# Attention, feed-forward layer and gated mixing on one core: conversion slots at 0.6 a step beside the second batch's attention, the next quarter's from the attention's end

## The chip, the cores and the metric

The kernel runs on one core of a Trainium2 chip. The metric is device time in microseconds (us): the median of the runs of the whole kernel. Work is done by five engines with a queue of instructions each, which they take in order: PE (TensorE, matrix products), DVE (VectorE), ACT (ScalarE), POOL (GpSimd) and SP, which here only starts transfers. An instruction that waits holds up everything behind it on its engine.

## The reference

B=2 batches, H=8 heads, S=768 positions, D=64, so a model width of 512. Three layers follow each other:

```
# 1 attention: window of 16 to each side, and a summary of each block of 32 keys
k_sum, v_sum = max and mean of k, v over each block of 32
scores = [q k^T / 8 where |i-j| < 16, else -1e9 ; q k_sum^T / 8 + log 32]
x = softmax(scores) [v ; v_sum]                  # (B, S, 512)
# 2 feed-forward, inner width 2048
u = x + (x^T U V)^T                              # U 768x32, V 32x768
x = u + relu(u w_ch1) w_ch2
# 3 gated mixing, inner width 1024, x_prev = x moved on by one position
xk, xr = mu_k x + (1-mu_k) x_prev, mu_r x + (1-mu_r) x_prev
out = sigmoid(xr w_r) * (relu(xk w_k)^2 w_v)
```

The weights lie in the memory of the chip as 64-bit floats and are brought to 32 bits on the chip.

## The kernel before, in words

**The order of the work.** The heads go in pairs n = 0 to 7. Pairs 0 to 3 are batch 0, pairs 4 to 7 batch 1. The attention of batch 0 fills the start (to about 54 us). Then the attention of batch 1 (`tail`) runs interleaved with the feed-forward layer of batch 0 over the first quarter of the inner width (`first_units`; `both` takes two steps of the attention for one of the feed-forward). This ends near 126 us. Then comes the first quarter for batch 1 alone (to 168 us), the quarters q = 1 to 3 for both batches (to about 364 us), and the third layer.

**The feed-forward layer.** A quarter has four blocks i of 128 inner columns, and each batch two chunks c of 384 positions. `f1` (L494) makes hidden block i: 12 matmuls (L506), a relu on ACT that gives the high part hh (L512), and on DVE the low part hl (L514), which is put in `hid_late` and emitted at the next `hid_flush`. `f2` (L520) multiplies hidden block i into four accumulators (L532); after the quarter's last block DVE adds them to y (L540, L543), and POOL adds the low part of u (`y_rest`, L308). Each product is made of three: high part by high, high by low, low by high. f1 and f2 each give way once in the middle (`yield`) and once at the end; a piece of six matmuls between two such points is called a step.

**The conversions.** Each weight block of 128 x 512 comes from memory as pairs of 32-bit words and passes five stages (`conv_jobs`, L399): s1 two ACT instructions (L423, L424), s2 three on DVE (L429, L432, L433), s3 an add on POOL (L439), s4 the high part whi on ACT (L464), s5 the low part wlo (L468), on DVE or POOL as the block says (`put_w`, `quarter_blocks`). In the first quarter DVE makes the low parts of all four blocks of w_ch2 and of blocks 2 and 3 of w_ch1; in the others POOL makes them all. A load goes on SP's queue. The stages stand in slots of a list `side`: a slot is one call that emits the next stages of the blocks under way, and a block takes two slots. The blocks of the first quarter are named below w1.0 to w1.3 and w2.0 to w2.3.

**What sets the order around the change.** There is no scheduler: the engines' queues hold what the Python code emits, in its order. `run(gen, rate)` (L744) walks a chain of steps and takes `rate` slots from `side` after each. In the attention a table `plan` (L316 to L397) says at which tick which part is emitted; its entries are "k" (`k_prep`: block maxima ks of the keys on DVE, L137, and the key windows kw on POOL, L143 to L145), "sv" (`sum_v`: block sums vs on DVE, L153; L158 on PE turns them, ACT copies them out at L160, POOL into vcat at L161), "d" (take slots from `side`), "u" (the feed-forward layer's input u, with its low part ulo on DVE, L301), and others. `drain(side)` without a number empties the list at once.

```
    run(both(first, tail, 2, 1), 1.0)
    for _ in tail:
        pass
    drain(side)
    ...
    side.extend(conv_jobs(quarter_blocks(1, wb_p)))
    run(chain(ffn_unit(0, 1, 0), ffn_unit(0, 1, 1)), 0.6)
    drain(side)
```

## Time and profile before

| what | value |
|---|---|
| time, median of 3 runs | 540.93 us (539.65 to 541.06) |
| time of the profiled execution | 540.89 us |
| its span, first to last instruction | 539.1 us |
| mean granted clock of PE | 0.991 |
| busy: PE, DVE, ACT, POOL | 515.4, 317.6, 250.4, 203.4 us |
| PE on the chain that ended last | 79% of the span |

The sum below is made against the profiled execution's own time, 540.89 us, of which 1.8 us lie around the span; it stands 0.04 us under the median of the runs. A busy PE can be at full or at half its clock: the granted clock of a stretch is 1.00 or 0.50, or between when the stretch holds both; the two levels are 2.4 and 1.2 GHz.

### The profile page before, as it was taken

To read this page: it belongs to the slowest core of one execution; us is meant where nothing else is said; L and a number is where in the kernel's file an instruction comes from. 1 tells how busy PE (TensorE), PEld (TensorE's weight loads), DVE (VectorE), ACT (ScalarE), POOL (GpSimd) and SP (SyncE) were. 2 spreads that over 40 slices of the span, in tenths; PEclk is the share of its full clock that TensorE was granted. 3 is DMA by queue.
4 is the path that set the end of the run, shared out by engine and by line. 5 is a ranking of instruction groups with operands and counts; after the bars stand their busy time and mean duration, and the time that the engine had idled before them with its cause. 6 is when DMAs were issued, how large, how long until landed. Compare 5 with 4: busy or idle time off the path is not lost.

```text
span 539.1 us, 8921 instructions
## 1 busy us (share of the span) xinstructions
PE 515.4 (96%) x3468; PEld 471.1 (87%) x3468; DVE 317.6 (59%) x706; ACT 250.4 (46%) x532; POOL 203.4 (38%) x184
## 2 busy tenths in 40 slices
PE   5889799999998999999999999999999999999997
PEld 4567577789998999999999999999888888888885
DVE  5995996444684486747775366565867443542222
ACT  4985674533451345524453254543566533532221
POOL 6553543032668166635765064232532120120000
PEclk9989898999999999999999999999999999999999
DMA  8995530400332133323433032021201000100101
GB/s 310 307 318 135 197 104 0 126 1 1 117 125 71 40 118 117 122 74 110 126 117 118 0 119 79 0 79 39 79 0 39 21 1 9 51 0 1 60 0 58
DMA packets 15129, 45.71 MB, mean 85 GB/s; under 512 B 2656, under 2 KB 2912, under 8 KB 15088
## 3 DMA queue, kind: packets, MB, share of 16 engines
q1 hardware_dynamic: 14912, 44.92, 25.2%
q8 instruction: 27, 0.44, 0.3%
q10 hardware_dynamic: 144, 0.18, 0.2%
q14 instruction: 14, 0.11, 0.1%
q0 software_dynamic: 32, 0.05, 0.0%
HBM read 42.00 MB, written 3.15 MB: 84 GB/s over the span
## 4 chain that ended last, share of the span: by engine, by line
PE 79%; DVE 10%; ACT 3%; DMA 3%; POOL 3%; issue 1%; SPq 0%; DVEq 0%; ACTq 0%; POOLq 0%
PE acc L532 23%; PE gen L506 22%; PE gen L648 12%; PE acc L670 12%; PE gen L632 5%; DMA stg<-vb 2%; PE gen L240 1%; DVE A L433 1%; POOL A L439 1%; DVE C L432 1%; DVE P L212 1%; DVE C L429 1%; DMA kt<-kt 1%; POOL wlo L468 1%; PE gen L227 1%
## 5 line engine op out<-in xcount | busy, mean ns | idle before, releaser
L439 POOL TENSOR_TENSOR A<-C,A 128x512 int32<-128x512 int32 (+1 forms) x54 | 71.4, 1322 | 89.2 <-DVE A L433 87.3
L532 PE MATMUL acc<-hh,whi 128*128 128x384 f32 x256 | 87.9, 343 | 2.6 <-DVE y L540 2.6
L506 PE MATMUL gen<-uhi,whi 128*128 128x384 f32 x256 | 87.8, 343 | 1.2 <-DVE hl L514 0.8
L506 PE MATMUL gen<-uhi,wlo 128*128 128x384 f32 x256 | 86.9, 340 | 0.0
L506 PE MATMUL gen<-ulo,whi 128*128 128x384 f32 x256 | 86.9, 340 | 0.0
L532 PE MATMUL acc<-hh,wlo 128*128 128x384 f32 x256 | 86.5, 338 | 0.0
L532 PE MATMUL acc<-hl,whi 128*128 128x384 f32 x256 | 86.5, 338 | 0.0
L468 POOL TENSOR_TENSOR wlo<-A,whi 128x512 fp32r<-128x512 f32 x46 | 68.0, 1478 | 37.4 <-ACT whi L464 37.3
L512 ACT ACTIVATE hh<-gen 128x384 fp32r<-128x384 f32 x64 | 31.3, 490 | 108.5 <-PE gen L506 108.4
L514 DVE SCALAR_TENSOR_TENSOR hl<-gen,hh 128x384 fp32r<-128x384 f32 x64 | 35.5, 555 | 65.0 <-ACT hh L512 65.0
L652 DVE TENSOR_TENSOR kt<-kt 128x384 f32<-128x384 f32 x32 | 20.3, 635 | 64.6 <-ACT kt L651 64.6
L433 DVE SCALAR_TENSOR_TENSOR A<-stg,A 128x512 int32<-128x512 int32 (+1 forms) x54 | 55.9, 1036 | 0.0
L532 PEld LDWEIGHTS acc<-hh,whi 128*128 128x128 f32 x256 | 48.1, 188 | 4.5 <-ACT hh L512 2.1
L506 PEld LDWEIGHTS gen<-uhi,whi 128*128 128x128 f32 x256 | 48.4, 189 | 2.8 <-DVE hl L514 1.4
L506 PEld LDWEIGHTS gen<-ulo,whi 128*128 128x128 f32 x256 | 48.5, 189 | 0.3 <-DVE ulo L301 0.3
L506 PEld LDWEIGHTS gen<-uhi,wlo 128*128 128x128 f32 x256 | 48.6, 190 | 0.0
L532 PEld LDWEIGHTS acc<-hl,whi 128*128 128x128 f32 x256 | 48.1, 188 | 0.0
L532 PEld LDWEIGHTS acc<-hh,wlo 128*128 128x128 f32 x256 | 48.1, 188 | 0.0
L464 ACT CAST whi<-A 128x512 fp32r<-128x512 f32 x52 | 32.2, 620 | 27.5 <-POOL A L439 27.3
L429 DVE TENSOR_SCALAR C<-C 128x512 f32<-128x512 f32 (+1 forms) x54 | 30.5, 565 | 23.0 <-ACT C L424 21.7
L648 PE MATMUL gen<-xkl,whi 128*128 128x384 f32 x128 | 43.2, 338 | 0.6 <-POOL xkl L610 0.6
L648 PE MATMUL gen<-xkh,whi 128*128 128x384 f32 x128 | 43.2, 337 | 0.0
(127 smaller groups left out, 985.8 us busy)
## 6 DMA issues: line engine op xcount, KB each, us to landing
stg<-w SPq DMA_DIRECT2D x32, 512.0 KB, 3.3
stg<-wk SPq DMA_DIRECT2D x8, 512.0 KB, 3.3
stg<-wv SPq DMA_DIRECT2D x8, 512.0 KB, 3.3
vcat<-vw SPq DMA_DIRECT2D x7, 585.0 KB, 4.7
kt<-kt SPq DMA_DIRECT2D x8, 384.0 KB, 5.3
vt<-vt SPq DMA_DIRECT2D x8, 384.0 KB, 5.7
out<-sig SPq DMA_DIRECT2D x12, 256.0 KB, 2.1
qt<-qt SPq DMA_DIRECT2D x7, 384.0 KB, 6.2
```

Of the source, the lines that this page charges most:

```text
L429: nc_v.tensor_scalar(out=c_f, in0=c_f, scalar1=as_float(0x38000000), scalar2=as_float(0x47EFFE00), op0=ALU.max, op1=ALU.min)
L433: nc_v.scalar_tensor_tensor(out=a, in0=st[i]["raw"][:, :, 1], scalar=-2 ** 31, in1=a, op0=ALU.bitwise_and, op1=ALU.bitwise_or)
L439: nc_p.tensor_tensor(out=a, in0=c, in1=a, op=ALU.add)
L464: nc_s.copy(wt[key][0], w)
L468: eng.tensor_tensor(out=lo, in0=w, in1=hi.bitcast(F32), op=ALU.subtract)
L506: nc_t.matmul(ps, w[:, sl], x[:, k], start=(n == 0), stop=(n == 3 * KD - 1))
L512: nc_s.activation(hh, ps, AF.Relu)
L514: lambda: nc_v.scalar_tensor_tensor(out=hl, in0=ps, scalar=0.0, in1=hh.bitcast(F32), op0=ALU.max, op1=ALU.subtract)
L532: nc_t.matmul(acc[d], w[:, sl], x, start=(i == 0 and n == 0), stop=(i == FT - 1 and n == 2))
L632: nc_t.matmul(ps, x[:, k, sl], w, start=(n == 0), stop=(n == 3 * KD - 1))
L648: nc_t.matmul(ps, w[:, sl], x[:, k], start=(n == 0), stop=(n == 3 * KD - 1))
L670: nc_t.matmul(acc, x[:, sl], w, start=(f == 0 and n == 0), stop=(f == KFT - 1 and n == 2))
```

## The change

In the attention of batch 0, the two single slots at ticks 10 and 11 move into the hand-written end of that attention, one ahead of u of pair 2 (`m`) and one behind the key preparation of pair 4, which itself moves there with its `sum_v`. Beside the attention of batch 1 the rate falls from 1.0 to 0.6 slots a step, and the list is not emptied at its end. The conversions of the second quarter are queued in `end_attention`, so that they follow in the same list without a gap, and what is left at the end of a quarter runs over into the next; the list is emptied once, after the last quarter. So that a block can't be read before it is converted, `f1` and `f2` call `ready`, which takes slots until the low part of their block has been emitted. `hold` stops the taking of slots in the second half of a unit's last `f2`. The low parts of w2.0 to w2.3 move from DVE to POOL. `hid_flush` runs at every step. `y_rest` of the first quarter goes between the conversions of quarter 2, whose rate is 0.75 in place of 0.5.

```diff
-    "g2", n), ("u", m, 1), ("fl",), ("ffn",), ("u", n, 0), ("u", n, 1), ("fl",),
+    ("t", n, 2), ("v", n, 1), ("g2", m), ("fl",), ("v", n, 2), ("fl",), ("d", 1), ("u", m, 0), ("g", n),
+    ("k", n + 1), ("d", 1), ("ffn",), ("g2", n), ("u", m, 1), ("fl",), ("sv", n + 1), ("ffn",), ("u", n, 0),
+    ("u", n, 1), ("fl",),
...
-                (10, (("lt", 5), ("d", 1))), (11, (("lv", 4), ("d", 1))),
-                (12, (("lv", 5), ("k", 4), ("sv", 4))),
+                (10, (("lt", 5),)), (11, (("lv", 4),)),
+                (12, (("lv", 5),)),
...
             eng.tensor_tensor(out=lo, in0=w, in1=hi.bitcast(F32), op=ALU.subtract)
+            done.add(key)
...
             res.append(block("w1", f, ("w1", f), pool, nc_v if q == 0 and i > 1 else nc_p))
-            res.append(block("w2", f, ("w2", f), pool, nc_v if q == 0 else nc_p))
+            res.append(block("w2", f, ("w2", f), pool))
...
     def f1(q, b, c, i, keep=False):
         hid_flush()
+        ready(("w1", q * FT + i))
...
     def f2(q, b, c, i):
         hid_flush()
+        ready(("w2", q * FT + i))
...
             if d == 2:
+                hold[0] = i == FT - 1
                 yield
...
+        hold[0] = False
         if i == FT - 1:
...
-                    side.append(lambda b=b, c=c, d=d: y_rest(b, c, d))
+                    rest.append(lambda b=b, c=c, d=d: y_rest(b, c, d))
...
+    def ready(key):
+
+        while key not in done:
+            drain(side, 1)
...
     def run(gen, rate):
         due = 0.0
         for _ in gen:
+            hid_flush()
             due += rate
-            while due >= 1.0:
+            while due >= 1.0 and not hold[0]:
...
     def end_attention():
         a_p.release()
         pools["y", 1] = tc.alloc_tile_pool(name="y1", bufs=1, side="right")
+        pools["wb"] = tc.alloc_tile_pool(name="wb", bufs=16, side="right")
         y_stage(1)
+        side.extend(conv_jobs(quarter_blocks(1, pools["wb"])))
...
-    run(both(first, tail, 2, 1), 1.0)
+    run(both(first, tail, 2, 1), 0.6)
     for _ in tail:
         pass
-    drain(side)
...
-    side.extend(conv_jobs(quarter_blocks(1, wb_p)))
     run(chain(ffn_unit(0, 1, 0), ffn_unit(0, 1, 1)), 0.6)
-    drain(side)
     for q in range(1, FQ):
...
-            side.extend(conv_jobs(blocks + [wk_block(4 * (q - 1) + f) for f in range(4)]))
-            run(chain(*units), 0.5)
+            for k, job in enumerate(conv_jobs(blocks + [wk_block(4 * (q - 1) + f) for f in range(4)])):
+                side.append(job)
+                if q == 2 and k % 2 and rest:
+                    side.append(rest.pop(0))
+            if q == 2:
+                side.extend(rest)
+            run(chain(*units), 0.5 if q == 1 else 0.75)
...
-        drain(side)
+    drain(side)
```

PE's order is the same in both kernels; what moves is what the other engines do for it. Three places show it. Line numbers of the changed kernel are a few higher (L439 becomes L440, L468 becomes L470, L532 becomes L538, L464 becomes L466, L512 becomes L516).

DVE where the first batch's attention ends and the second's begins (near 54 us), before:

```order
L280 TENSOR_TENSOR gst<-acc,gst 32x128
L301 TENSOR_TENSOR ulo<-acc,uhi 128x384 x4
L137 TENSOR_REDUCE ks<-kt_111 128x24
L153 TENSOR_REDUCE vs<-vt_113 128x24
L429 TENSOR_SCALAR C<-C 128x512
L432 TENSOR_SCALAR C<-C 128x512
L433 SCALAR_TENSOR_TENSOR A<-stg,A 128x512
L514 SCALAR_TENSOR_TENSOR hl<-gen,hh 128x384
L468 TENSOR_TENSOR wlo<-A,whi 128x512
L514 SCALAR_TENSOR_TENSOR hl_944<-gen,hh_943 128x384
L212 ISA P,nm<-gen,mask 128x120
```

and after:

```order
L430 TENSOR_SCALAR C<-C 128x512
L433 TENSOR_SCALAR C<-C 128x512
L434 SCALAR_TENSOR_TENSOR A<-stg,A 128x512
L137 TENSOR_REDUCE ks<-kt_111 128x24
L280 TENSOR_TENSOR gst<-acc,gst 32x128
L301 TENSOR_TENSOR ulo<-acc,uhi 128x384 x2
L153 TENSOR_REDUCE vs<-vt_113 128x24
L301 TENSOR_TENSOR ulo<-acc,uhi 128x384 x2
L518 SCALAR_TENSOR_TENSOR hl<-gen,hh 128x384
L518 SCALAR_TENSOR_TENSOR hl_938<-gen,hh_937 128x384
L430 TENSOR_SCALAR C<-C 128x512
L433 TENSOR_SCALAR C<-C 128x512
```

The two reductions of pair 4 (L137, L153) now stand between the parts of u, a conversion's three instructions ahead of them, and no low part (L468) is left here.

POOL at the last pair of the attention (near 107 us), before; here wlo_1344 of w2.3 doesn't occur, because DVE makes it:

```order
L439 TENSOR_TENSOR A_1153<-C_1154,A_1153 128x512
L439 TENSOR_TENSOR A_1234<-C_1235,A_1234 128x512
L161 COPY vcat0_104<-vm_1398 24x24x64
L143 COPY kw1_109<-kt1_111 128x12x32
L144 COPY kw1_109<-kt1_111 128x12x64
L145 COPY kw1_109<-ks_1407 128x12x24
L161 COPY vcat1_105<-vm_1610 24x24x64
L311 TENSOR_TENSOR y_919<-y_919,ulo_593 128x384 x4
```

and after; wlo_1492 is that of w2.2, wlo_1591 that of w2.3:

```order
L145 COPY kw1_109<-ks_1389 128x12x24
L440 TENSOR_TENSOR A_1319<-C_1320,A_1319 128x512
L470 TENSOR_TENSOR wlo_1492<-A_1319,whi_1491 128x512
L440 TENSOR_TENSOR A_1422<-C_1423,A_1422 128x512
L161 COPY vcat1_105<-vm_1609 24x24x64
L470 TENSOR_TENSOR wlo_1591<-A_1422,whi_1590 128x512
L306 MEMSET y_1853 128x4
```

On PE the readers stand in the changed kernel as follows (the same places as before, where the tiles are called gen_1608 and wlo_1344):

```order
L538 MATMUL acc_1141<-hh_1256,wlo_1492 128x384
L275 MATMUL gen_1602<-g4_1544,stack_97 96x128
L158 MATMUL gen_1607<-ident_90,vs_1546 24x128
L538 MATMUL acc_1138<-hh_1459,whi_1590 128x384
L538 MATMUL acc_1138<-hl_1460,whi_1590 128x384
L538 MATMUL acc_1138<-hh_1459,wlo_1591 128x384
```

The copy into vcat (L161) reads what comes from gen_1607 (L158), and POOL makes wlo_1591 behind this copy; PE reads wlo_1591 two matmuls behind L158.

ACT at the end of the first quarter (about 160 to 168 us), before:

```order
L464 CAST whi<-A 128x512
L512 ACTIVATE hh<-gen 128x384
L423 ACTIVATE A<-stg 128x512
L424 ACTIVATE C<-stg 128x512
L464 CAST whi<-A 128x512 x2
L512 ACTIVATE hh<-gen 128x384 x5
```

and after:

```order
L424 ACTIVATE A<-stg 128x512
L425 ACTIVATE C<-stg 128x512
L516 ACTIVATE hh<-gen 128x384
L466 CAST whi<-A 128x512
L516 ACTIVATE hh<-gen 128x384 x2
L466 CAST whi<-A 128x512
L516 ACTIVATE hh<-gen 128x384 x2
```

The two high parts that stood together, ahead of five relus, now stand apart with relus between them.

## Rows read from the trace of the kernel before

**Rows 1.** The page, busy time of the engines over the whole execution.

```profile
PE 515.4 (96%) x3468; PEld 471.1 (87%) x3468; DVE 317.6 (59%) x706; ACT 250.4 (46%) x532; POOL 203.4 (38%) x184
```

**Rows 2.** Windows: length, busy (count) of PE, PEld, DVE, ACT, POOL; granted clock; DMA.

```profile
27.00:40.50 13.50, 11.62 (x158) 8.38 (x158) 13.06 (x54) 11.69 (x32) 7.63 (x6) 0.87 0.92 319
54.00:62.00 8.00, 5.26 (x62) 3.41 (x61) 7.36 (x25) 4.51 (x11) 5.11 (x6) 1.00 0.50 178
62.00:66.00 4.00, 3.73 (x26) 2.93 (x26) 3.97 (x15) 2.11 (x7) 1.82 (x2) 0.57 0.50 175
66.00:82.00 16.00, 13.62 (x154) 10.97 (x155) 14.93 (x54) 13.00 (x32) 6.96 (x7) 1.00 0.36 121
148.00:170.00 22.00, 19.37 (x110) 18.79 (x109) 16.20 (x26) 9.97 (x18) 16.29 (x13) 1.00 0.37 120
170.00:360.00 190.00, 190.00 (x1086) 189.99 (x1085) 116.92 (x195) 81.61 (x153) 93.06 (x71) 1.00 0.26 84
```

**Rows 3.** Windows, same columns: the stretches around two falls of the clock.

```profile
58.50:62.20 3.70, 2.00 (x35) 1.43 (x35) 3.09 (x20) 1.76 (x5) 2.38 (x3) 1.00 0.98 361
62.20:65.60 3.40, 3.40 (x26) 2.73 (x24) 3.37 (x13) 1.71 (x6) 1.82 (x2) 0.50 0.41 137
79.00:82.70 3.70, 2.14 (x25) 1.57 (x25) 3.63 (x15) 2.43 (x7) 1.27 (x1) 0.99 0.28 87
82.70:86.00 3.30, 3.30 (x26) 2.44 (x29) 2.22 (x5) 0.29 (x2) 0.00 (x0) 0.50 0.00 0
```

**Rows 4.** Groups by line, DVE, 53.5 to 91 us: busy, mean ns | idle.

```profile
L468 DVE TENSOR_TENSOR wlo<-A,whi 128x512 fp32r<-128x512 f32 x6 | 6.7, 1123 | 0.0
L137 DVE TENSOR_REDUCE ks<-kt 128x24 f32<-128x768 f32 x4 | 3.8, 947 | 0.0
L433 DVE SCALAR_TENSOR_TENSOR A<-stg,A 128x512 int32<-128x512 int32 x5 | 3.7, 741 | 0.0
L432 DVE TENSOR_SCALAR C<-C 128x512 int32<-128x512 int32 x5 | 3.4, 681 | 0.2
L429 DVE TENSOR_SCALAR C<-C 128x512 f32<-128x512 f32 x5 | 2.1, 420 | 0.3 <-ACT C L424 0.3
```

**Rows 5.** Waits of PE, 53 to 100 us: total, times, longest.

```profile
PE gen L200 <- POOL kw L145: 0.7, 1, 0.7
```

**Rows 6.** Groups by line on POOL, whole execution.

```profile
L439 POOL TENSOR_TENSOR A<-C,A 128x512 int32<-128x512 int32 x53 | 70.2, 1325 | 89.1 <-DVE A L433 87.3 <-PE gen L648 1.0 <-PE acc L532 0.6
L468 POOL TENSOR_TENSOR wlo<-A,whi 128x512 fp32r<-128x512 f32 x46 | 68.0, 1478 | 37.4 <-ACT whi L464 37.3
```

**Rows 7.** Timeline (start, us, engine): last block's low part, its first reader.

```profile
87.32 0.69 DVE L468 TENSOR_TENSOR wlo<-A,whi 128x512 fp32r<-128x512 f32 x1
...
106.24 0.40 PE L158 MATMUL gen<-ident,vs 128*24 128x128 f32 x2
106.68 0.27 ACT L160 ACTIVATE vm<-gen 24x128 f32<-24x128 f32 x1
107.02 0.33 PE L532 MATMUL acc<-hh,wlo 128*128 128x384 f32 x1
107.08 1.47 POOL L161 COPY vcat<-vm 24x1536 f32<-24x1536 f32 x1 [12.95 <-ACT vm L160]
```

**Rows 8.** Timeline of the stops at the end of the first quarter.

```profile
149.76 0.41 PE L532 MATMUL acc<-hh,whi 128*128 128x384 f32 x1 [0.84 <-DVE y L540]
...
166.32 0.62 ACT L464 CAST whi<-A 128x512 fp32r<-128x512 f32 x1 [2.68 <-POOL A L439]
166.85 0.86 ACT L512 ACTIVATE hh<-gen 128x384 fp32r<-128x384 f32 x2
...
168.53 0.42 PE L532 MATMUL acc<-hh,whi 128*128 128x384 f32 x1 [1.79 <-DVE y L540]
```

**Rows 9.** Timeline: one DVE instruction beside one of POOL.

```profile
153.97 1.30 POOL L439 TENSOR_TENSOR A<-C,A 128x512 int32<-128x512 int32 x1 [1.42 <-DVE A L433]
154.14 1.41 DVE L429 TENSOR_SCALAR C<-C 128x512 f32<-128x512 f32 x1 [0.25 <-ACT C L424]
```

More of the change, by code (lines that the diff above doesn't have):

```diff
@@ L352, in attention @@
                 (end, (
-                    ("t", n, 2), ("v", n, 1), ("g2", m), ("fl",), ("v", n, 2), ("fl",), ("u", m, 0), ("g", n), ("ffn",),
-                    ("g2", n), ("u", m, 1), ("fl",), ("ffn",), ("u", n, 0), ("u", n, 1), ("fl",),
+                    ("t", n, 2), ("v", n, 1), ("g2", m), ("fl",), ("v", n, 2), ("fl",), ("d", 1), ("u", m, 0), ("g", n),
+                    ("k", n + 1), ("d", 1), ("ffn",), ("g2", n), ("u", m, 1), ("fl",), ("sv", n + 1), ("ffn",), ("u", n, 0),
+                    ("u", n, 1), ("fl",),
                 )),
@@ L459, in build @@
     wt = {}
+    done = set()
     def put_w(key, pool, eng=nc_p):
@@ L540, in f2 @@
                     nc_v.tensor_tensor(out=yd, in0=acc[d], in1=u_t[b, c][0][:, d].bitcast(F32), op=ALU.add)
-                    side.append(lambda b=b, c=c, d=d: y_rest(b, c, d))
+                    rest.append(lambda b=b, c=c, d=d: y_rest(b, c, d))
                 else:
                     nc_v.tensor_tensor(out=yd, in0=acc[d], in1=yd, op=ALU.add)
+    rest = []
     prev = [None]
+    hold = [False]
+    def ready(key):
+        while key not in done:
+            drain(side, 1)
     def ffn_unit(q, b, c):
@@ L773, in both @@
                 next(other, None)
+            hid_flush()
             yield
-    run(both(first, tail, 2, 1), 1.0)
+    run(both(first, tail, 2, 1), 0.6)
     for _ in tail:
         pass
-    drain(side)
     x_p.release()
-    wb_p = tc.alloc_tile_pool(name="wb", bufs=16, side="right")
+    wb_p = pools["wb"]
     wk_p = tc.alloc_tile_pool(name="wk", bufs=16, side="right")
```

## The prediction, made before the changed kernel ran

> **What bounds the kernel now.** The first view is the busy time of the engines. PE is busy for 96% of the span [rows 1], so the kernel can become faster only where PE stands still or runs at half its clock; DVE, ACT and POOL have much time free on the mean. The second view is the windows, which show that this mean hides two kinds of stage. From 170 to 360 us PE has no idle time at all, at a granted clock of 1.00 [rows 2]: nothing can be won there, and there is only cover to lose. At the end of batch 0's attention (27 to 40.5 us) and in the stage after it (54 to 82 us) DVE is the full engine: 13.06 of 13.5 us, then 7.36 + 3.97 + 14.93 = 26.26 of 28 us, while PE is idle for 8.00 - 5.26 = 2.74, 4.00 - 3.73 = 0.27 and 16.00 - 13.62 = 2.38 us, together 5.39 us [rows 2]. Third, the clock. After 3.7 us in which PE was busy for 2.00 us the granted clock is 0.50 for the next 3.4 us, and after 3.7 us with 2.14 us busy it is 0.50 for 3.3 us [rows 3]. This is the lower of its two levels, 1.2 GHz in place of 2.4, so such a stretch gives back half its length, 1.7 us, if it goes. Last, the end of the first quarter: PE is idle for 22.00 - 19.37 = 2.63 us between 148 and 170 us [rows 2], and the timeline names two stops, 0.84 and 1.79 us [rows 8].
>
> A difference of 0.3%, 1.6 us, is about what a measurement of this kernel can tell from none.
>
> **The change part by part**, against the profiled execution's 540.89 us, which is 0.04 us under the median.
>
> *A, the end of the first batch's attention.* Two slots leave ticks 10 and 11. Of what they emitted DVE loses one trio (L429, L432, L433): 0.42 + 0.68 + 0.74 = 1.84 us [rows 4], out of a stretch in which DVE is busy for 97% and PE waits. It returns further down, in the hand-written end stage, where it stands ahead of the key reduction of pair 4. Ends: 0, if it only delays that stage instead, and -1.84. I take -1.5, near the upper end, because DVE has 0.44 us free in the stretch that it leaves and not more.
>
> *B, relief of DVE from 54 to 82 us.* By the lower rate and the move to POOL, DVE loses there five low parts of 1.12 us, one trio of 1.84 us, and the two reductions of pair 4, of about 0.95 us each, which now come earlier: 5.6 + 1.84 + 1.9 = 9.35 us out of 26.26 [rows 2, 4]. PE idles 5.39 us there, and the two halved stretches cost 1.7 us each, so at most 8.8 us can be won; nothing, if PE's waits only pass on to ACT or POOL. I take -5.4: about 3.7 us of the idle time, two thirds, since some of it is the chain from scores to softmax to values, which has no slack however free DVE is, and one of the two clock falls, 1.7 us.
>
> *C, the key windows of pair 6.* On POOL one add of a conversion (1.325 us [rows 6]) now stands ahead of the copies L143 to L145. PE already waited 0.7 us for these once [rows 5]. Ends 0 and +1.3; I take +0.5, because DVE's reduction in front of the copies ends sooner by B.
>
> *D, the low part of w1.3.* It stays on DVE (1.12 us [rows 4]) but is emitted by the lower rate just ahead of its first reader, behind the scores of the pair. Ends 0 and +2.2, two such instructions; I take +1.1, one.
>
> *E, the low part of w2.3.* Before, DVE made it at 87.32 us, some 19 us before its first reader at 107.02 us. Now it is on POOL behind the copy into vcat. That copy began at 107.08 us and took 1.47 us, since it waits for ACT's copy (106.68 us), which waits for a matmul (106.24 us) that stands two matmuls ahead of the reader [rows 7]. With 1.48 us for the low part on POOL [rows 6] it ends at 107.08 + 1.47 + 1.48 = 110.03 us, and PE stands for 3.0 us. The queue behind it is PE's whole. Ends 2.6, if the copy is a little earlier, and 3.5. A gap of 3.0 us is longer than the 1.7 us and the 1.6 us that PE lacked in the two stretches before the falls [rows 3], so I add a clock fall of 1.7 us; ends 0 and 1.7. Together +4.7.
>
> A sentence apart: the Trainium skill (GPSIMD Engine Reference, Key points) says that VectorE is about twice as fast as GpSimd in elementwise work; the rows give 1478 to 1123 ns, a factor of 1.3 [rows 4, 6], and by the page's factor, as an estimate, the low part would take 2.25 us and the wait would be 3.8 us in place of 3.0.
>
> *F, the end of the first quarter.* Emptying the list put high parts (L464, 0.62 us, waiting 2.68 us for POOL) ahead of the relus on ACT, and PE then stood for 1.79 us until the accumulators were added to y; the stop of 0.84 us comes from DVE work of a conversion ahead of the same adds one chunk earlier [rows 8]. With no emptying there and no slots taken in the last half of a unit's last f2, both can go: ends 0 and -2.63. I take -2.2, since a slot taken one step earlier can still stand ahead of the second chunk's adds.
>
> *G, the rest at nothing.* The second quarter's conversions start earlier, `y_rest` moves, and quarter 2 has a higher rate. All this lies between 126 and 360 us, where PE has no idle time and POOL is busy for 93.06 of 190 us [rows 2], so half of POOL and more of ACT cover it. SP's loads move by one place at most and DMA is 0.26 busy there. If the cover is gone, a block that comes late costs its low part, 1.5 us.
>
> Sum: -1.5 - 5.4 + 0.5 + 1.1 + 4.7 - 2.2 = -2.8, so 540.89 - 2.8 = **538.1 us**.
>
> **The rivals.**
>
> *R1, the relief is whole and the clock stands.* B gives its upper end, -8.8, and after the wait for w2.3 no fall comes (E +3.0): -1.5 - 8.8 + 0.5 + 1.1 + 3.0 - 2.2 = -7.9, **533.0 us**. For it: DVE is at 94% and the relief of 9.35 us is larger than the idle time. Against: the softmax chain's own latency.
>
> *R2, POOL beside DVE gives half of the relief back.* One DVE instruction (L429), 0.42 us on the mean, took 1.41 us when an add of POOL ran beside it [rows 4, 9]. Four low parts move to POOL, into a stage where it was busy for 5.11 of 8 us at the start [rows 2]. If B is only half, 2.7 us, the sum is -0.1, **540.8 us**. Against: in most of the stage POOL was busy for less than half. The Trainium skill (GPSIMD Engine Reference, Key points) states that the two engines share their access to SBUF and contend for some DVE instructions; by that rule R2 is the likelier, and the 1.41 us agrees with it.
>
> *R3, slower: low parts that come just in time.* The lower rate brings each of the first quarter's last low parts near its reader, not only the two of D and E. If w1.2 waits as w1.3 does (+1.1) and w2.2 as w2.3 does (+4.7, with a fall of the clock), the sum is -2.8 + 5.8 = +3.0, **543.9 us**. It decides from the point where w2.2's low part, which on POOL is behind the key copies of pair 7 and one more add, ends after PE has gone through that pair's scores. For it: four conversions are late by a rate of 0.6 in place of 1.0. Against: between those copies and the reader PE has two groups of scores and a whole f1, over 4 us, and the add and the low part take 1.325 + 1.48 = 2.8 us [rows 6].
>
> *R4, the change does not do what it says at the quarter's end.* The stops at 150 and 168 us stay, because the conversions of a list without a gap stand ahead of the relus and adds as before: F is 0, the sum -0.6, **540.3 us**. For it: the high parts on ACT still stand among the last relus, now apart. Against: they no longer follow each other, and none has to be emitted out of turn.
>
> **How the numbers follow.** The forecast's sum has 0.45, of which 0.37 is below 539.3 us (faster by over 1.6 us) and 0.08 above it; R1 has 0.25, R2 0.13, R4 0.05, R3 0.12. Faster: 0.37 + 0.25 = 0.62. Same: 0.08 + 0.13 + 0.05 = 0.26. Slower: 0.12. The range goes from R1's 533.0, less 0.5 for the upper ends of A and F, to 542.5, between R2 and R3, so that it leaves out the upper half of R3 and the lower edge of R1: 532.5 to 542.5. The likeliest case's own range is 536 to 540.5.
>
> **What would show it right or wrong.** A: from 27 to 54 us PE gets through the same work about 1.5 us sooner. B: between the first batch's end and pair 6, DVE's busy share falls from 94% to about two thirds, PE's idle time from 5.4 to below 2 us, and of the halved stretches one is left. C: the wait of PE for L145 grows from 0.7 to over 1 us. E: one wait of PE of about 3 us for wlo, L470 on POOL, near 105 us, and half clock behind it. F: the waits of 0.84 and 1.79 us for y (L540 before) shrink to under 0.5 us together. G: PE idle 0 through quarters 1 to 3. Wrong it would be above all if PE's idle time near 54 to 82 us does not fall though DVE is free (the bound was the softmax chain), or if waits for low parts show up in more places than one.

## The result: slower, and the profile after

The changed kernel takes 547.09 us (median of 4 runs, 545.83 to 549.13) where the kernel before takes 540.29 us (median of 4, 539.13 to 541.06): a ratio of 1.0128, 95% interval 1.0103 to 1.0154. The prediction said 538.1 us, faster, and a range of 532.5 to 542.5; the result lies outside, on the other side. The profiled execution is the fastest of the four (545.83 us, span 544.0 us, mean granted clock 0.994); the three others have 0.986, 0.986 and 0.981, so that some 1.3 us of the median stand in no row below.

Busy time on the page of the changed kernel, to be read against [rows 1]:

```profile
PE 515.0 (95%) x3468; PEld 469.8 (86%) x3468; DVE 330.3 (61%) x702; ACT 252.6 (46%) x532; POOL 210.9 (39%) x188
```

PE does the same work. POOL has 7.5 us more, of which the four low parts that it took over are 5.9 (4 x 1.48). DVE has four low parts less, and yet 12.7 us more.

The windows of [rows 2] for the changed kernel (columns as there; its work at a given time is up to 4 us further on or back):

```profile
54.00:62.00 8.00, 4.34 (x49) 3.27 (x42) 7.26 (x29) 1.95 (x6) 3.95 (x5) 0.89 0.53 184
62.00:66.00 4.00, 4.00 (x34) 3.51 (x33) 1.98 (x10) 2.71 (x8) 1.97 (x2) 0.79 0.00 0
66.00:82.00 16.00, 14.35 (x181) 11.39 (x182) 13.31 (x44) 10.70 (x28) 7.57 (x7) 1.00 0.46 146
148.00:170.00 22.00, 21.96 (x126) 21.67 (x125) 16.94 (x28) 10.08 (x19) 15.54 (x11) 1.00 0.39 133
170.00:360.00 190.00, 186.37 (x1060) 185.01 (x1059) 128.63 (x187) 81.30 (x149) 101.80 (x79) 1.00 0.24 81
```

Three things are to be seen. Between 148 and 170 us PE's idle time fell from 2.63 to 0.04 us, as forecast. Between 54 and 62 us PE is idle for longer than before, 3.66 against 2.74 us, and DVE is as full as before. And from 170 to 360 us, where PE had no idle time, it now has 3.63 us.

The waits of PE over the whole execution, behind the one for the first load, name the places:

```profile
PE gen L200 <- DVE nm L212: 4.2, 4, 2.8
PE acc L538 <- DVE y L550: 3.6, 2, 2.2
PE acc L538 <- POOL wlo L470: 2.8, 1, 2.8
...
PE gen L200 <- POOL kw L145: 1.4, 1, 1.4
PE gen L510 <- DVE wlo L470: 1.1, 1, 1.1
```

The wait for L145 grew from 0.7 [rows 5] to 1.4 us, as C had it.

Since PE's order is the same in both kernels, each matmul has its counterpart. The table gives how much later (+) or earlier (-) it starts in the changed kernel, counted from the first instruction of each. The third quarter is the one that the prediction calls quarter 2 (q = 2).

| start of the matmul before, us | place | changed kernel | step since the line above |
|---|---|---|---|
| 53.10 | end of batch 0's attention | -1.53 | -1.53 (A) |
| 59.22 | pair 4, first scores | -3.70 | -2.17 |
| 66.11 | pair 4 | -1.65 | +2.05 |
| 90.13 | pair 6 | -3.90 | -2.25 (with the two above B and C, -2.37) |
| 98.03 | behind the first reader of w1.3 | -2.53 | +1.37 (D) |
| 106.57 | just ahead of the reader of w2.3 | -2.55 | -0.02 |
| 112.08 | behind it | +1.97 | +4.52 (E) |
| 145.27 | first quarter, batch 1 | +1.97 | 0 |
| 172.11 | second quarter | -0.85 | -2.82 (F) |
| 262.14 | third quarter | -0.47 | +0.38 |
| 300.13 | third quarter | +3.61 | +4.08 |
| 430.11 | third layer | +4.93 | +1.32 (the last three G, +5.78) |

The table compares one execution of each kernel, and the half clock falls differently from one execution to the next: before at 28.0 to 31.5, 62.2 to 65.6 and 82.7 to 86.1 us, in the changed kernel at 60.3 to 63.7 and 108.0 to 111.5 us. So its sizes are not sharp. Twelve of the kernels of the experiments have the changed kernel's order up to 53.10 us, and there they stand between -1.55 (e3) and +0.62 us (e5). Five of them (e1, e2, e9, e13, e14) have one stretch of about 3.4 us at half clock near 28 us, like the kernel before, and stand between -0.97 and -1.34 us. For B and C together e1, e2 and e14, whose order is the changed kernel's up to 181 us, give -1.3 to -1.8 us.

The first big loss, E, in the timeline (start, duration, engine, line, what ended the idle time before it):

```profile
104.12 0.27 ACT L160 ACTIVATE vm<-gen 24x128 f32<-24x128 f32 x1
104.53 1.46 POOL L161 COPY vcat<-vm 24x1536 f32<-24x1536 f32 x1 [4.99 <-ACT vm L160]
106.07 1.26 POOL L470 TENSOR_TENSOR wlo<-A,whi 128x512 fp32r<-128x512 f32 x1
...
107.39 0.44 PE L538 MATMUL acc<-hh,wlo 128*128 128x384 f32 x1 [2.75 <-POOL wlo L470]
```

POOL was idle for 4.99 us, held by the copy's wait with the low part behind it, then did both, and PE stood for 2.75 us; 3.5 us at half clock follow, from about 108 us.

The second, at pair 4's first scores:

```profile
54.20 1.47 POOL L161 COPY vcat<-vm 24x1536 f32<-24x1536 f32 x1 [2.51 <-ACT vm L160]
54.28 1.67 DVE L430 TENSOR_SCALAR C<-C 128x512 f32<-128x512 f32 x1
55.74 0.58 POOL L143 COPY kw<-kt 128x384 f32<-128x384 f32 x1
55.99 0.61 DVE L433 TENSOR_SCALAR C<-C 128x512 int32<-128x512 int32 x1
56.27 1.01 POOL L144 COPY kw<-kt 128x768 f32<-128x768 f32 x1
56.52 1.30 DVE L434 SCALAR_TENSOR_TENSOR A<-stg,A 128x512 int32<-128x512 int32 x1
57.74 0.27 DVE L212 CUSTOM_DVE_ANT_0 P<-gen,mask 128x120 f32<-128x120 f32 x1
...
58.57 0.64 PE L200 MATMUL gen<-kw,qt 64*64 64x120 f32 x16 [2.79 <-DVE nm L212]
```

The trio that took 1.84 us [rows 4] takes 1.67 + 0.61 + 1.30 = 3.58 us, because each of its three instructions meets a copy on POOL; the masked scores (L212), for which PE waits, are behind it on DVE.

The third, at the end of a unit in quarter 2:

```profile
286.59 1.28 POOL L440 TENSOR_TENSOR A<-C,A 128x512 int32<-128x512 int32 x1 [0.62 <-DVE A L434]
286.90 1.25 DVE L430 TENSOR_SCALAR C<-C 128x512 f32<-128x512 f32 x1
288.19 0.43 DVE L433 TENSOR_SCALAR C<-C 128x512 int32<-128x512 int32 x1
288.54 0.68 DVE L434 SCALAR_TENSOR_TENSOR A<-stg,A 128x512 int32<-128x512 int32 x1
289.14 1.94 DVE L550 TENSOR_TENSOR y<-acc,y 128x384 f32<-128x384 f32 x4
289.84 0.41 PE L538 MATMUL acc<-hh,whi 128*128 128x384 f32 x1 [2.17 <-DVE y L550]
```

DVE came to the four adds to y only after a whole trio, and PE, which needs the accumulators again, stood for 2.17 us.

### The profile page after: what moved, and what is told of

It reads as the page before. It is cut to its first block, busy times and chain, and to the rows that moved or that the text cites. A ratio compares the mean times of both kernels' runs of the same rounds, so it can differ in the third digit from the quotient of the medians.

```text
span 544.0 us, 8898 instructions
## 1 busy us (share of the span) xinstructions
PE 515.0 (95%) x3468; PEld 469.8 (86%) x3468; DVE 330.3 (61%) x702; ACT 252.6 (46%) x532; POOL 210.9 (39%) x188
## 4 chain that ended last, share of the span: by engine, by line
PE 73%; DVE 9%; POOL 5%; ACT 5%; DMA 4%; issue 3%; SPq 0%; POOLq 0%; DVEq 0%; ACTq 0%
PE gen L510 21%; PE acc L538 21%; PE acc L685 11%; PE gen L663 10%; PE gen L647 5%; POOL A L440 2%; DMA stg<-vb 2%; POOL wlo L470 2%; DVE C L430 2%; DVE A L434 1%; PE gen L200 1%; PE gen L240 1%; DVE C L433 1%; DVE P L212 1%; PE gen L227 1%
## 5 line engine op out<-in xcount | busy, mean ns | idle before, releaser
L440 POOL TENSOR_TENSOR A<-C,A 128x512 int32<-128x512 int32 (+1 forms) x54 | 72.2, 1337 | 82.2 <-DVE A L434 71.1
L538 PE MATMUL acc<-hh,whi 128*128 128x384 f32 x256 | 88.5, 346 | 3.7 <-DVE y L550 3.6
L538 PE MATMUL acc<-hh,wlo 128*128 128x384 f32 x256 | 86.9, 340 | 2.8 <-POOL wlo L470 2.8
L470 POOL TENSOR_TENSOR wlo<-A,whi 128x512 fp32r<-128x512 f32 x50 | 74.1, 1483 | 35.4 <-ACT whi L466 35.3
L538 PE MATMUL acc<-hl,whi 128*128 128x384 f32 x256 | 86.7, 338 | 0.0
L516 ACT ACTIVATE hh<-gen 128x384 fp32r<-128x384 f32 x64 | 31.3, 488 | 74.3 <-PE gen L510 73.9
L466 ACT CAST whi<-A 128x512 fp32r<-128x512 f32 x52 | 32.3, 621 | 49.8 <-POOL A L440 49.6
L538 PEld LDWEIGHTS acc<-hh,whi 128*128 128x128 f32 x256 | 48.3, 189 | 6.6 <-issue 5.2
L538 PEld LDWEIGHTS acc<-hh,wlo 128*128 128x128 f32 x256 | 48.2, 188 | 3.1 <-POOL wlo L470 3.1
L538 PEld LDWEIGHTS acc<-hl,whi 128*128 128x128 f32 x256 | 48.3, 189 | 0.0
L424 ACT ACTIVATE A<-stg 128x512 f32<-128x512 uint32 (+1 forms) x54 | 36.3, 671 | 25.9 <-DMA stg<-w 15.1
L433 DVE TENSOR_SCALAR C<-C 128x512 int32<-128x512 int32 (+1 forms) x54 | 42.3, 784 | 1.9
```

The costliest lines, as they stand in the source:

```text
L424: nc_s.activation(a, raw_[:, :, 0].bitcast(U32), AF.Copy, scale=2.0 ** -51, bias=2.0)
L433: nc_v.tensor_scalar(out=c, in0=c, scalar1=3, scalar2=None, op0=ALU.logical_shift_left)
L440: nc_p.tensor_tensor(out=a, in0=c, in1=a, op=ALU.add)
L466: nc_s.copy(wt[key][0], w)
L470: eng.tensor_tensor(out=lo, in0=w, in1=hi.bitcast(F32), op=ALU.subtract)
L516: nc_s.activation(hh, ps, AF.Relu)
```

## The experiments

The ratios are to the kernel before, measured beside each group of runs on the same chip (540.74 us for e1 to e4, 540.94 for e5 to e8, 541.10 for e9 to e12, 540.39 for e13 and e14); differences in us to the changed kernel are of medians. The theory after the result: the loss has three places, each with too much on one engine's queue (POOL's at w2.3, POOL and DVE at pair 4, POOL and DVE in quarter 2). The rivals were that the overrun of the list or the rate of 0.6 costs by itself.

**e1_spread: quarter 2's load spread over two quarters.**

```diff
-                if q == 2 and k % 2 and rest:
+                if k % 3 == 2 and rest:
-            run(chain(*units), 0.5 if q == 1 else 0.75)
+            run(chain(*units), 0.62)
```

> The changed kernel, with y_rest of the first quarter spread over the second and third quarter (one behind every third conversion slot, in place of one behind every second in the third quarter alone) and both at 0.62 slots a step. Theory (load): in quarter 2 a block has 2 slots at 0.75, some 2.8 us, and POOL needs 1.34 + 1.48 + 0.9 = 3.7 us for its add, its low part and a y_rest, so DVE's conversion falls behind and stands ahead of the y adds. With the load spread, the stops of 1.5 and 2.2 us near 270 and 290 us go, and nothing comes for them: about 4 us less than the changed kernel, a span near 540. Rival (no emptying): the stops come from conversions that run over the quarter's end and so meet the last adds of a unit whatever their rate; then stops of together 2 to 4 us stay, at other places, and the span stays within 1.5 us of 544.

Measured: 546.56 us, ratio 1.0097 (1.0064 to 1.0131). Its profiled run took 543.79 us, and in its trace both stops of quarter 2 are gone: from 262.14 to 300.13 us the matmuls' delay doesn't change. But PE waits 2.1 us for y at the third layer's start, where 5 slots are emitted at once, and at pair 4 it loses 1.1 us more than the changed kernel to a longer stretch at half clock, though the order there is the same. The theory holds at its place; the span of 542.0 us missed the 540 expected.

**e2_q2_rate: quarter 2 at 0.5**, `y_rest` left there (`0.5 if q == 1 else 0.75` becomes `0.5`).

> The changed kernel with the third quarter's rate at 0.5 in place of 0.75, y_rest left where it is. Theory (load): the two stops of quarter 2 go as in the spread version, since a block has 4.2 us; but 19 slots in place of 4 are left at the end of the last quarter and are emitted at once ahead of the third layer, which costs 0 to 4 us there. Rival (no emptying): the stops of quarter 2 stay. PE's idle time from 210 to 310 us tells the two apart: under 0.5 us by the theory, over 2 us by the rival.

Measured: 558.15 us, ratio 1.0327 (1.0295 to 1.0358). No stop in quarter 2; the 19 slots left over cost 16.6 us between 362 and 376 us, far more than the 0 to 4 us expected. The waits of PE from 355 to 400 us, to which a fall of the clock came:

```profile
PE acc L685 <- DVE y L550: 10.0, 1, 10.0
PE gen L663 <- POOL xkl L625: 1.2, 2, 0.6
```

**e3_w2lo_dve: w2's low parts back on DVE.**

```diff
-            res.append(block("w2", f, ("w2", f), pool))
+            res.append(block("w2", f, ("w2", f), pool, nc_v if q == 0 else nc_p))
```

> The changed kernel with the low parts of w2.0 to w2.3 back on DVE. Theory (POOL's queue): PE's wait of 2.8 us for POOL's low part near 107 us and the half clock behind it go, 4.5 us together, of which a wait for DVE of up to 1.1 us comes back because the slot is still emitted just ahead of the reader: 3.4 to 4.5 us less than the changed kernel, a span near 540. Rival (relief of DVE): with four low parts of 1.1 us back on DVE between 54 and 107 us, the 2.0 to 2.7 us that the changed kernel wins between 62 and 90 us are lost again, and the sum is only 1 to 2 us less than the changed kernel.

Measured: 544.17 us, ratio 1.0072 (1.0051 to 1.0094), 2.9 us under the changed kernel, a little less than the 3.4 to 4.5 expected. Loss E shrinks from 4.52 to 0.80 us (from -2.75 to -1.95 us over the same matmuls), and what was won up to pair 6 is not lost (-4.45 against -3.90 us), so taking these low parts off DVE had won nothing. Part of it goes again in quarter 2, whose stops are 1.4 us longer.

**e4_attn_rate1: 1.0 slots a step beside the attention, as before** (`0.6` becomes `1.0` in `run(both(...))`).

> The changed kernel with 1.0 slots a step beside the second batch's attention, as before. Theory (just in time): no block is emitted at its reader any more, so the waits for the low parts of w1.3 (1.1 us) and w2.3 (2.8 us, and 1.7 us of half clock) go, 5.6 us; the conversions come earlier and load DVE again between 54 and 90 us, which costs up to 2.5 us: 3 to 5.6 us less than the changed kernel. Rival (a full DVE): the rate of 0.6 was needed, DVE is as full as before between 54 and 82 us and POOL's copies stretch its conversions besides, so that more than 4 us are lost there and the time is within 1.5 us of the changed kernel's.

Measured: 538.57 us, ratio 0.9963 (0.9947 to 0.9979), 8.5 us under the changed kernel and more than expected. Undoing this one number makes the change a gain. The waits of PE from 50 to 126 us:

```profile
PE gen L240 <- issue: 2.2, 1, 2.2
PE gen L200 <- DMA qt<-qt: 1.9, 1, 1.9
PE gen L200 <- DVE nm L212: 0.9, 1, 0.9
PE gen L200 <- POOL kw L145: 0.7, 1, 0.7
...
```

No wait for a low part is left, and the longest for L212 is 0.9 us.

**e5_rate1_spread: e4 with e1's spread, and 0.7 in place of 0.6 in the last quarter**, so that no slot is left at its end.

> The changed kernel with 1.0 slots a step beside the second batch's attention, y_rest spread over the second and third quarter at 0.62 a step, and the last quarter at 0.7 in place of 0.6, so that no slot is left ahead of the third layer. Theory (three sources of loss, each of them load at one place): the just-in-time low parts go by the rate, the stops of quarter 2 by the spread, the one at the third layer's start by the empty list: another 2 us under the kernel with the rate alone (538.57 us), so 536 to 537. Rival (phase: which conversion meets which unit's end is chance): the stops move to other unit ends, and the time is within 1 us of 538.6 or above.

Measured: 535.66 us, ratio 0.9907 (0.9880 to 0.9934), a little under what was expected. The 2.8 us that e4 loses between 262 and 300 us are 0.6 here.

**e6_vcat_act: the copy into vcat on ACT** (`nc_p.tensor_copy` becomes `nc_s.copy` in `spread_v`).

> The changed kernel with the copy into vcat on ACT in place of POOL, all else as it is. Theory (POOL's queue and POOL beside DVE): near 107 us POOL's low part of w2.3 no longer stands behind this copy, so PE's wait falls from 2.8 us to at most 1.5 us; near 54 us the first instruction of a conversion on DVE, which took 1.67 us beside this copy, takes 0.4 to 0.7 us, and PE's stop for the scores (2.8 us) falls to 1.5 to 2.0 us. Together 2 to 4 us less than the changed kernel. Rival (the slot itself is late): the low part waits for its own high part and the stop near 107 us stays over 2.3 us; the DVE instruction near 54 us stays over 1.3 us, because it is not the copy that holds it.

Measured: 547.99 us, ratio 1.0130 (1.0107 to 1.0154), no gain in all. At both places the theory holds: the wait for w2.3 is gone, and the trio ahead of pair 4's scores takes 0.42 + 0.43 + 0.69 us. But in batch 0's attention, where ACT was busy for 11.69 of 13.5 us before [rows 2], the kernel lost 7.0 us (by 53.10 us, against the changed kernel), with half clock from 23.5 to 37 us.

**e7_rate1_w2lo_dve: e4 and e3 together.**

> The changed kernel with 1.0 slots a step beside the attention and the low parts of w2.0 to w2.3 on DVE, both as before; what is left of the change are the attention's plan, the list that is not emptied, and quarter 2. Theory (relief of DVE is worth something once nothing is just in time): 1.5 to 3 us slower than with the rate alone, 540 to 541.5, with the time lost between 54 and 90 us. Rival (the relief is worth nothing, since the scores' chain sets that stage): within 0.8 us of 538.57.

Measured: 536.65 us, ratio 0.9928 (0.9900 to 0.9957). Not slower than e4 (0.9963) but 1.9 us faster, which the rival did not have either. So the theory fell: low parts off DVE are worth nothing, at this rate too. Why it is faster was not tested; its profiled execution has no stretch at half clock, that of e4 one of 6.9 us near 28 us, where the order is the same.

**e8_rate1_plan_before: e4 with the first attention's plan as before.**

> The changed kernel with 1.0 slots a step beside the attention, and the first attention's plan as before (slots at ticks 10 and 11, key preparation and sum of pair 4 at tick 12). Theory (the plan's edits are worth 1.5 to 2 us at the end of the first attention): 1 to 2.5 us slower than with the rate alone, lost between 30 and 60 us. Rival (the first attention's half-clock stretch decides and the edits only move it): within 0.8 us of 538.57.

Measured: 540.51 us, ratio 1.0001 (0.9986 to 1.0017), 1.9 us over e4, as expected. At 53.10 us, where step A is read, the two traces are level (e8 +0.18, e4 +0.07 us, but e4 with 6.9 us at half clock near 28 us and e8 with none); e4 gains 2.0 us on e8 between there and 59.22 us. The edit also takes back the earlier key preparation of pair 4, which the prediction counts under B. So e8 shows what the plan's edits are worth together, 1.9 us, and not A alone.

**e9_vcat_act_b1: e6 for pairs 4 to 7 alone.**

```diff
-        nc_p.tensor_copy(vcat[n % 2][KW:KC, :, :, 0:D], vm[KW:KC].unsqueeze(1).to_broadcast([NB, NT, 2, D]))
+        (nc_s.copy if n >= 4 else nc_p.tensor_copy)(
+            vcat[n % 2][KW:KC, :, :, 0:D], vm[KW:KC].unsqueeze(1).to_broadcast([NB, NT, 2, D])
+        )
```

> The changed kernel with the copy into vcat on ACT for pairs 4 to 7 alone, at the slow rate of 0.6. With the copy on ACT for all pairs, the first attention lost 6.9 us and the second won 2.9 + 1.5 us near 107 us and 3.6 us between 54 and 65 us. Theory (POOL's queue, and POOL beside DVE's conversions): with the first attention left alone the wins stay, 6 to 8 us less than the changed kernel, so 539 to 541. Rival (the gain came from the later start, in which the conversions were further on): 3 us or less, 544 and above.

Measured: 539.76 us, ratio 0.9973 (0.9953 to 0.9992), 7.3 us under the changed kernel at the same slow rate (8.4 by the ratios). The timeline at the two places (lines are two higher):

```profile
54.35 1.47 ACT L161 COPY vcat<-vm 24x1536 f32<-24x1536 f32 x1
54.53 0.42 DVE L432 TENSOR_SCALAR C<-C 128x512 f32<-128x512 f32 x1
54.98 0.43 DVE L435 TENSOR_SCALAR C<-C 128x512 int32<-128x512 int32 x1
55.32 0.68 DVE L436 SCALAR_TENSOR_TENSOR A<-stg,A 128x512 int32<-128x512 int32 x1
...
101.52 1.27 POOL L472 TENSOR_TENSOR wlo<-A,whi 128x512 fp32r<-128x512 f32 x1 [3.40 <-ACT whi L468]
102.25 0.40 PE L158 MATMUL gen<-ident,vs 128*24 128x128 f32 x2
102.98 1.48 ACT L161 COPY vcat<-vm 24x1536 f32<-24x1536 f32 x1
103.03 0.33 PE L540 MATMUL acc<-hh,wlo 128*128 128x384 f32 x1
```

The same copy, as long as before, stands beside the trio on ACT now, and the trio takes 1.53 us in place of 3.58. The low part of w2.3 is ready 0.24 us before its reader.

**e10_spread_w2lo_dve: e5 with w2's low parts on DVE.**

> The best kernel so far (1.0 slots a step beside the attention, y_rest spread at 0.62 a step, the last quarter at 0.7) with the low parts of w2.0 to w2.3 on DVE as before. Theory (taking low parts off DVE is worth nothing, since DVE's conversions are shorter where POOL has less beside them): within 1.5 us of 535.66. Rival (the relief is worth 1.5 us or more once the rest is in order): 537 or above.

Measured: 536.02 us, ratio 0.9898 (0.9876 to 0.9920), the same as e5.

**e11_spread_vcat_act: e5 with e9's copies.**

> The best kernel so far (1.0 slots a step, spread, 0.7) with the copy into vcat on ACT for pairs 4 to 7. Theory (POOL beside DVE's conversions): 0.5 to 2 us less than 535.66, won between 54 and 90 us. Rival (at this rate no conversion stands beside the copy ahead of the scores, so nothing is won, and ACT is held 1.5 us by each copy): 535.2 or above.

Measured: 537.12 us, ratio 0.9914 (0.9890 to 0.9938), the rival: at this rate nothing is won.

**e12_no_hold: e5 without hold** (the line `hold[0] = i == FT - 1` left out).

> The best kernel so far without hold, so that slots are also taken in the second half of a unit's last f2. Theory (conversions ahead of the adds to y are what stops PE at a unit's end): one or more of the fourteen unit ends of the four quarters gets a stop of 0.8 to 2 us again, 1 to 4 us slower than 535.66 in all. Rival (only the emptied list made the stops at the end of the first quarter): within 0.8 us.

Measured: 539.10 us, ratio 0.9956 (0.9940 to 0.9972), 3.4 us over e5. Against that of e5 its trace loses 0.6 to 0.9 us at each of four unit ends, near 199, 216, 268 and 331 us, and next to nothing (0.2 us) at the end of the first quarter. The longest waits of PE from 126 us on:

```profile
PE acc L537 <- DVE y L549: 1.4, 2, 1.0
PE acc L537 <- ACT C L425: 0.7, 1, 0.7
```

So hold pays in the later quarters, and F, at the first quarter's end, does not rest on it. That leaves above all the list that is no longer emptied, of which 8 slots came at once there before; no run tested it by itself.

**e13_slow_repaired: the changed kernel at 0.6 with e9's copies, e1's spread and 0.7 in the last quarter.**

> The changed kernel at its rate of 0.6, with three repairs: the copy into vcat on ACT for pairs 4 to 7, y_rest spread over two quarters at 0.62 a step, the last quarter at 0.7. Theory (the rate costs only through the places found: POOL's queue at the last block, POOL beside DVE's conversion ahead of the scores, and the overfull quarter 2): all go, what is left against the repaired kernel at rate 1.0 (535.66 us) is the wait of 1.1 us for the low part of w1.3, so 535 to 538. Rival (the rate of 0.6 costs by itself, in places not found): 539 or above.

Measured: 535.19 us, ratio 0.9905 (0.9881 to 0.9930). Of the waits of PE over the whole execution, those for the scores and the one for a low part:

```profile
PE gen L202 <- DVE nm L214: 2.6, 5, 0.9
...
PE gen L512 <- DVE wlo L472: 1.1, 1, 1.1
```

The longest wait for the scores is 0.9 us in place of 2.8. e11 is this kernel at a rate of 1.0, and it is no faster (0.9914 against 0.9905): beyond the places found, the rate of 0.6 costs nothing that these two intervals can tell from none, the 1.1 us for w1.3 included.

**e14_spread_q3: e1 with 0.7 in the last quarter.**

> The changed kernel with y_rest spread at 0.62 a step and the last quarter at 0.7, nothing else. Theory (overfull quarter 2, and slots emptied at the third layer's start): the spread alone took 4.1 us off quarter 2 and gave back 1.5 us at the third layer's start, where 5 slots were left; with none left this comes to 4 to 6 us less than the changed kernel, 541 to 543. Rival (what the stops cost comes back as a half-clock stretch or a wait later): 545 or above, as with the spread alone (546.56).

Measured: 542.06 us, ratio 1.0029 (1.0018 to 1.0041), 5.0 us under the changed kernel. From 262 to 430 us it loses 0.15 us where the changed kernel loses 5.4. So e1's spread was right: 2.8 us of its missing gain stood at the third layer's start. Another 2.8 us lie between e1's profiled run and its median and stand in no trace (granted clock 0.990 and 0.984).

The two repairs alone give 7.3 us (e9) and 5.0 us (e14), together 12.3; e13 with both is 11.9 us under the changed kernel. By the ratios to the kernel before it is 1.55, 0.99 and 2.23%, or 8.4, 5.4 and 12.1 us, so that they add up to within 2 us. Together they take back more than the 6.8 us that the change had cost. The fastest kernels, e13, e5 and e10 (0.9905, 0.9907, 0.9898), can't be told apart.

## Why the prediction was wrong

By its own steps, in us, from the table above:

| step | predicted | measured | verdict |
|---|---|---|---|
| A, end of batch 0's attention | -1.5 | -1.5 | right, as far as one trace tells |
| B and C, relief of DVE, key windows | -4.9 | -2.4 | size wrong |
| D, low part of w1.3 | +1.1 | +1.4 | right |
| E, low part of w2.3 | +4.7 | +4.5 | right |
| F, end of the first quarter | -2.2 | -2.8 | right |
| G, "the rest at nothing" | 0 | +5.8 | wrong |
| sum | -2.8 | +4.9 | |

The step that turned the sign is **G**: up to 172.11 us the changed kernel was still 0.85 us ahead. G argued from the mean over 190 us, in which POOL is busy for 93.06 us, "so half of POOL and more of ACT cover it". That mean says nothing of quarter 2. There a `y_rest` takes a slot of its own, so a block with its `y_rest` takes three slots, four steps at 0.75 a step; a block alone took as many before, two slots at 0.5. With a step of 1.05 us (16 steps lie between the 266.47 and the 283.30 us at which the adds to y of two units begin before) that is 4.2 us. POOL's add, low part and `y_rest` took 1.39, 1.58 and 1.08 us on the mean between 253 and 269 us, 4.0 us together, and POOL and DVE have next to no room left there (the kernel before, then the changed kernel; columns as in [rows 2]):

```profile
253.00:269.00 16.00, 16.00 (x94) 16.00 (x93) 12.03 (x20) 8.82 (x16) 11.06 (x8) 1.00 0.44 131
253.00:269.00 16.00, 16.00 (x93) 15.86 (x92) 14.56 (x15) 6.94 (x14) 15.05 (x12) 1.00 0.28 87
```

POOL is busy for 15.05 of 16 us in place of 11.06; in e2 it is 10.66, in e1 13.67, in e14 12.63. (The reckoning in e1's expectation, 3.7 us of work in the 2.8 us of two slots, leaves out the slot of the `y_rest`; the cover was gone, but by less.) The trios come 4.6 to 5.0 us apart there, each later behind its slot, and PE stands at the unit's end. The place of the trio alone does not stop PE: one stands directly ahead of the adds to y at 249.33 us too, where POOL was busy for only 4.38 of the 15 us before; it took 0.42 + 0.43 + 0.69 us there, and PE did not wait. At 0.75 the stops are there in the changed kernel, e3 and e9, and smaller in e4; they are gone at 0.5 (e2) and at 0.62 (e1, e13, e14), but for 0.6 us in e5, e10 and e11. G also named the wrong price: the loss was not a late block but a whole trio ahead of the adds to y, at two unit ends, and after it slots left over at the third layer's start (+0.8).

The other step is **B**. Its clock term was right: of the two stretches at half clock between 54 and 90 us one is left. Its idle term of 3.7 us failed. The rows are for the same matmuls, from the one at 53.10 to the one at 90.13 us before, in the kernel before, in the changed kernel and in e9 (columns as in [rows 2]):

```profile
53.10:90.13 37.03, 31.65 (x326) 24.81 (x325) 32.72 (x108) 22.76 (x57) 14.41 (x15) 0.91 0.32 110
51.57:86.23 34.66, 29.36 (x326) 23.69 (x325) 26.50 (x97) 20.34 (x53) 13.62 (x15) 0.95 0.40 128
51.81:84.79 32.98, 29.86 (x325) 24.01 (x324) 24.05 (x97) 23.06 (x55) 11.35 (x15) 0.95 0.41 135
```

DVE was relieved of 6.2 us, less than the 9.35 counted, and PE's idle time did not fall: 5.38 us before, 5.30 after. The prediction had named this as the sign that would show it wrong, with the softmax chain as the bound; but in e9, where only the copy into vcat moves, it is 3.12 us, so 2.2 us of it were not that chain's. DVE's relief was counted in instructions at the durations of before. But the step that took the trio out of the first attention's end and slowed the rate put a trio beside POOL's copies of pair 4, ahead of the first scores, and there it took 3.58 us in place of 1.84. This is rival R2, "POOL beside DVE", which had a chance of 0.13 and named the stage, but was priced as half of the relief and sought in the low parts that move. The cause is the copy into vcat, which didn't move, with the key copies that it holds back: with it on ACT (e9) 2.0 us come back at this place and 1.7 are left of it at pair 6. The four low parts off DVE are worth nothing (e3, e7, e10). R3, the slower rival, had two more low parts arriving late; no such wait appeared beyond D and E.

DVE's longer busy time has the same cause. The conversions' three groups of DVE from 126 to 364 us in the kernel before,

```profile
L433 DVE SCALAR_TENSOR_TENSOR A<-stg,A 128x512 int32<-128x512 int32 x40 | 45.1, 1127 | 0.0
L429 DVE TENSOR_SCALAR C<-C 128x512 f32<-128x512 f32 x40 | 23.2, 580 | 21.7 <-ACT C L424 20.4 <-POOL A L439 1.3
L432 DVE TENSOR_SCALAR C<-C 128x512 int32<-128x512 int32 x40 | 21.0, 525 | 1.4
```

and in the changed kernel:

```profile
L434 DVE SCALAR_TENSOR_TENSOR A<-stg,A 128x512 int32<-128x512 int32 x38 | 42.0, 1104 | 0.0
L433 DVE TENSOR_SCALAR C<-C 128x512 int32<-128x512 int32 x38 | 30.2, 794 | 1.3
L430 DVE TENSOR_SCALAR C<-C 128x512 f32<-128x512 f32 x38 | 27.2, 716 | 3.6 <-ACT C L425 3.6
```

The two first instructions of the trio (L430, L433) are 23% and 51% longer on the mean, with the same work, and the three groups together take 99.4 us in place of 89.3, with two trios fewer. That alone stops nothing: in e13 they are as long (753 and 810 ns), and PE stands only where the trio is ahead of something that PE needs.

What stays open: the stretch at half clock near 60 us is 3.5 us long in the changed kernel and some 7 us in e1 and e14, whose order up to there is the same; at 66 us these two stand 1.1 and 1.3 us behind the changed kernel. The half clock near 28 us varies in the same way. No experiment controlled either.

## What to carry to other kernels

A mean over a long stage does not show cover: before a stage is put at nothing, the queue that feeds it is worked out for each rate, as time per slot against the work that one slot gives each engine, and with every list that takes slots counted in. A rate for filler work is bounded from both sides: too fast and it fills the queues ahead of what the main engine waits for, too slow and the last items come just in time, or pile up at the next point where the list is emptied; 0.6 cost 8.5 us here against 1.0, and nothing measurable once the copy and the later quarters were put right (e13 against e11). And before an instruction goes to another engine's queue, look at what it will stand behind: a copy with a wait on the main engine's last instruction, just ahead of the reader, was worth 4.5 us.

## What the runs showed of the hardware

A DVE instruction of a conversion that begins while POOL works makes hardly any progress until POOL is done. L430 began at 54.28 us beside a copy that ended at 55.67 us, and ended at 55.95 us; [rows 9] show the same (POOL's end at 155.27, DVE's at 155.55 us): 0.28 us behind POOL's end both times, where the whole instruction takes 0.42 us alone. In the changed kernel 22 instructions of L430 began with at least 0.1 us of one of POOL's still to run, and all ended 0.28 to 0.30 us behind its end. Ten others had begun before POOL's and took 0.41 to 0.42 us, as long as alone; so here it counts which of the two begins first. L430 met a copy that reads 24 partitions as it met an add over 128. The same copy on ACT (e9) leaves the instruction at 0.42 us. The masked scores on DVE (L212) show no such stretch here: at most 0.28 us beside POOL and alone.

The Trainium skill (Trainium Architecture — The Big Picture, What this means for kernel authors) says that the port pair shared by DVE and GpSimd is "an exclusive lock (not a bandwidth split)". These rows agree: the time that DVE lost beside the copy, 1.67 - 0.42 = 1.25 us, is nearly the 1.39 us in which the two ran side by side. By this rule R2 should have been priced as up to the full length of each POOL instruction that meets a conversion ahead of a wait of PE, 1.3 to 1.5 us each, and not as a share of the relief.

The other rule that the prediction weighed is that VectorE is about twice as fast as GpSimd in elementwise work (the Trainium skill, GPSIMD Engine Reference, Key points). The trace agrees where each ran alone: the low part took 0.69 us on DVE [rows 7] and 1.26 us on POOL near 107 us, a factor of 1.8. The means behind the prediction's factor of 1.3, 1.12 and 1.48 us, hold instructions that ran beside the other engine. Its estimate of 2.25 us, twice such a mean, was too long: the wait was 2.75 us, nearer to the 3.0 of the rows than to the 3.8 of the estimate.
